# A transformer block on one NeuronCore: 32-row head slots in the Q/K scratch, a DMA model of 16 engines, and an order searched offline

## The chip, the cores and the metric

The kernel runs on one core of a Trainium2 chip. It is written in Bass: the program says itself which instruction each engine runs, in which order, and on which semaphores it waits. The engines are TensorE (PE, matrix products; its weight loads have a row of their own, PEld), VectorE (DVE), ScalarE (ACT), GpSimd (POOL) and SyncE (SP), which here issues every DMA. The metric is the device time of one execution in microseconds (us).

## The reference

One block with sliding-window attention and a gated MLP; the layer norms are modulated by a vector `c`. 2048 rows, width 640, 32 heads of 20, a window of 256 keys, 1536 hidden units.

```python
mod = (silu(c) @ w_mod).reshape(1, 6, 1, 640)        # sa, ca, ga, sb, cb, gb
h = layernorm(x) * (1 + ca) + sa
qkv = h @ wqkv                                       # [2048, 3*640]: q, k, v of 32 heads x 20
scores = q @ k.T * 20 ** -0.5                        # per head
scores = where(0 <= i - j < 256, scores, -1e9)       # causal, sliding window
o = softmax(scores) @ v
x = x + ga * (o @ wo)
h = layernorm(x) * (1 + cb) + sb
x = x + gb * ((sigmoid(h @ w_gate) * (h @ w_up)) @ w_down)
```

## The kernel before

The Python code is a small list scheduler. Every piece of work is an operation `A(engine, function, duration, reads=..., writes=..., prio=..., tag=...)`; buffers are pools of slots that a `Tile` takes when its first operation is placed. `schedule()` simulates the engines with the durations given, takes at each step the operation that can start first (among those that can start within 0.13 of each other on TensorE, the one with the lowest `prio`), and so fixes each engine's order; `emit()` then writes that order with semaphore waits. Nothing is reordered on the chip: each engine runs its list, and waits where an operand is late. For a DMA the model is one shared pipe:

```python
            dur = o.dur[e]
            free[e] = st + dur
            if o.isdma:
                s0 = max(st + dur + 0.3, bw)
                move = o.nbytes / 330e3
                bw = s0 + move
                o.end = s0 + move + o.fix
```

The 2048 rows are 16 blocks of 128. Q, K and V are made in four chunks of four blocks (`cc`); attention, output projection and MLP run over six chunks `a` of 2, 2, 4, 4, 2 and 2 blocks. The buffers that matter here:

```python
    p_stg = sbpool("stg", 3, [128, 512])
    p_QT = sbpool("QT", 3, [128, 4, 512])
    p_KT = sbpool("KT", 4, [128, 4, 512])
    p_V = sbpool("V", 10, [128, H * VW + 10])
    p_E = sbpool("E", 4, [128, 4, 512])
    p_On = sbpool("On", 2, [128, 1024])
    p_oT = sbpool("oT", 1, [128, NDT, 512])
    p_big = sbpool("big", 1, [128, 6400])
# ... PSUM:
    p_S = Pool("S", [nc.alloc_psum_tensor("S0", [128, 4, 512], F32)])
    p_O = Pool("O", [nc.alloc_psum_tensor("O0", [128, 512], F32)])
    p_M = Pool("M", [nc.alloc_psum_tensor(f"M{i}", [128, 512], F32) for i in range(3)])
```

The vector `c` is loaded first, with its 640 values spread over 128 partitions, then x, `w_mod` and the Q/K/V weights:

```python
    dma(lambda: c_col[:], lambda: c.rearrange("o (t p) -> p (o t)", p=128), 1280, writes=[R_ccol], prio=0, nonc=True)
```

hT is the normed and modulated x with the features on the partitions. In chunk 0 TensorE transposes it; in chunks 1 to 3 a DMA transpose does, and VectorE modulates the result in place:

```python
        else:
            for bi in range(4):
                transp(t, src[bi], bi, 4)
            modulate(t, 512, 4, scA, shA, [R_mA], 12)
```

[...] For chunk 0 a *direct* projection makes them so: four heads go to four 32-column parts of the TensorE array, which work side by side (20 matmuls for each group of 4 heads, for each of q and k, for each half `hf` of the chunk):

```python
                    for k0, k1 in ((0, 1), (1, 2), (2, 3), (3, 4), (4, 5)):
                        def fn(e, eng, k0=k0, k1=k1, which=which, ps=ps, g_=g_):
                            for kt in range(k0, k1):
                                for j in range(4):
                                    c0 = kt * D + (4 * g_ + j) * DH
                                    ins = mm(e, ps.ap[32 * j:32 * j + 32, 0:256], wqk_t[which][:, c0:c0 + 32],
                                             hT[0].ap[:, kt, hf * 256:hf * 256 + 256], kt == 0, kt == NDT - 1,
                                             tp=(0, 32 * j))
```

For chunks 1 to 3 plain 128-row projections are used. The result (640 rows) is written to a DRAM scratch from a staging buffer `stg`, and read back with the heads spread out, four reads of 20 partitions each:

```python
    def proj_qk(cc, mts, halves, prio):
        for which, (w, Rw) in enumerate(((wq, R_wq), (wk, R_wk))):
            key = "qk"[which]
            if (cc, which) not in dq:
                dq[(cc, which)] = (dram(f"d{key}{cc}", [D, 512]), [R(f"d{key}{cc}_{m}") for m in range(NDT)])
            dt_, Rd = dq[(cc, which)]
            for mt in mts:
                ps = Tile(p_M, f"{key}{cc}_{mt}")
                pairs = [(lambda kt=kt, mt=mt, w=w, ps=ps: (ps.ap[:], w[:, kt, mt * 128:(mt + 1) * 128],
                                                            hT[cc].ap[:, kt, :])) for kt in range(NDT)]
                s = Tile(p_stg, f"stg{key}{cc}_{mt}")
                pe_chain(ps, 512, pairs, [Rw + [hT[cc].r(kt)] for kt in range(NDT)], prio, f"proj{key}{cc}", hold=[s])
                evac(lambda s=s: s.ap[:], lambda ps=ps: ps.ap[:], 512, [ps.r()], [s.r()], 6, "evqk")
                dma(lambda mt=mt, d=dt_: d[mt * 128:(mt + 1) * 128, :], lambda s=s: s.ap[:], 131072, reads=[s.r()],
                    writes=[Rd[mt]], prio=2, fix=0.9, tag="qkw")
            for hh in halves:
                t = Tile((p_QT, p_KT)[which], f"{key}T{cc}_{hh}")
                (QT, KT)[which][(cc, hh)] = t
                lo, hi = 320 * hh // 128, (320 * hh + 319) // 128
                for j in range(4):
                    dma(lambda j=j, t=t: t.ap[32 * j:32 * j + DH, :, :],
                        lambda j=j, hh=hh, d=dt_: d.rearrange("(g r) c -> r g c", r=4 * DH)[
                            j * DH:(j + 1) * DH, 4 * hh:4 * hh + 4, :], 81920,
                        reads=[Rd[m] for m in range(lo, hi + 1)], writes=[t.r(j)], prio=2, k=10, tag="qkr")
```

Attention goes over the 8 groups of 4 heads. `pieces_of` cuts a group's (key block, query block) pairs into sets of at most four 128-column blocks; one set is one score run on TensorE (into the single score buffer S), one exp on ScalarE, masks of its diagonal and far blocks on GpSimd, and one PV run on TensorE, placed later and in pairs:

```python
    def pieces_of(i0, QB):
        ps = []
        for kb in range(max(0, i0 - 2), i0 + QB):
            q0, q1 = max(kb, i0), min(kb + 2, i0 + QB - 1)
            ps.append((kb, q0, q1 - q0 + 1))
        ps.sort(key=lambda x: (-x[2], x[0]))
        sets = []
        for p in ps:
            for s in sets:
                if sum(y[2] for y in s) + p[2] <= 4:
                    s.append(p)
                    break
            else:
                sets.append([p])
        return sets
        ...
        for g in range(NG):
            hh, gl = g // 4, g % 4
            gpo = 512 // W
            if g % gpo == 0:
                O = Tile(p_O, f"O{a}_{g}")
            first = [True] * 4
            qt = QT[(cc, hh)]
            for si, st in enumerate(sets):
                E = Tile(p_E, f"E{a}_{g}_{si}")
                ...
                    for (kb, q0, n) in st:
                        kt = KT[(kb // 4, hh)]
                        for j in range(4):
                            ins = mm(e, Sp.ap[:, j, off:off + n * 128],
                                     kt.ap[32 * j:32 * j + DH, gl, (kb % 4) * 128:(kb % 4) * 128 + 128],
                                     qt.ap[32 * j:32 * j + DH, gl, (q0 % 4) * 128:(q0 % 4 + n) * 128],
                                     True, True, tp=(32 * j, 0))
```

`norm` transposes the accumulator O with VectorE, divides by the softmax sums and transposes back into On. On then goes to a DRAM scratch `doc` in four stores, one for each head of a group, and comes back as oT in one read:

```python
        out_r = []
        for j in range(4):
            Rj = R(f"doc{a}_{g0}_{j}")
            dma(lambda j=j: doc.rearrange("(g r) c -> r g c", r=4 * DH)[j * DH:(j + 1) * DH, g0:g0 + G, :],
                lambda j=j: On.ap[32 * j:32 * j + DH, :].rearrange("p (g c) -> p g c", g=G), 40960,
                reads=[On.r(0), On.r(1)], writes=[Rj], prio=1, k=10, fix=0.9, tag="n_ow")
            out_r.append(Rj)
        return out_r
# ... and after the last group:
        oT = Tile(p_oT, f"oT{a}")
        dma(lambda: oT.ap[:, :, 0:W], lambda: doc.rearrange("(t p) c -> p t c", p=128), D * W * 2, reads=R_doc,
            writes=[oT.r()], prio=2, tag="oT")
```

The output projection and the MLP follow; `qkv` orders the projections:

```python
    def qkv(cc):
        if cc == 0:
            proj_qk_direct(0, 12)
            proj_v(0, 12.35)
            proj_qk_direct(1, 13.6)
        else:
            proj_qk(cc, (0, 1, 2), (0,), 20 + cc)
            proj_v(cc, 20 + cc)
            proj_qk(cc, (3, 4), (1,), 20 + cc)
# ... the MLP of one chunk, 12 tiles of hidden units, gate and up (W is 256 or 512), then down:
        for ft in range(NFT):
            pg, pu, sg = Tile(p_M, "g"), Tile(p_M, "u"), Tile(p_sig, "sig")
            for ps, w, tg in ((pg, 0, "g"), (pu, 1, "u")):
                pairs = [(lambda kt=kt, ft=ft, ps=ps, w=w: (ps.ap[:, 0:W], wgu[:, w, kt, ft * 128:(ft + 1) * 128],
                                                            h2.ap[:, kt, 0:W])) for kt in range(NDT)]
# ...
                    ps.ap[:, 0:320], hv(ft)[:, bi * 128:(bi + 1) * 128], wd[:, ft, half * 320:half * 320 + 320]))
                    for ft in range(NFT)]
```

The softmax here doesn't subtract the row's maximum and nothing guards it: scores larger than these inputs give would overflow.

## Time and profile before

| | |
|---|---|
| time, median of 3 | 361.11 us (359.8 to 361.29) |
| span of the profiled execution | 358.6 us |
| mean granted TensorE clock | 0.995 |
| exps on ScalarE (128 partitions x 2048, 1536, 1024 elements) | 72, 8 and 24 |
| exp of 128x2048 | 1.876 us |
| direct projection matmuls | 640 |
| DMA packets | 52672, of which 22544 under 512 B |
| moved by DMA | 40.32 MB |

In the profile a line such as `L521` names the line of the kernel; L521 and L522 are the two branches of the matmul helper, without and with a tile position, so that L522 is scores (`S`), PV (`O`) and direct projections. `dq`, `dk` and `doc` are the DRAM scratches, `wgu` and `wd` the MLP weights, `big` the MLP's hidden units (and, early, `w_mod`). A group of instructions shows how many there were, their busy time and the mean time of one, and after a second bar the idle time of the engine just before them, with what ended it. A wait shows total us, how often, and the longest.

The chain that ended last, by share of the span:

```profile
PE 71%; DMA 9%; DVE 7%; SPq 4%; ACT 3%; issue 3%; POOL 1%; DVEq 0%; POOLq 0%
```

The busy time by stage (window, length, then PE, PEld, DVE, ACT and POOL busy with their instructions, clock, DMA share, GB/s):

```profile
0.00:9.00 9.00, 6.40 (x38) 2.83 (x39) 3.61 (x10) 1.49 (x2) 4.30 (x33) 1.00 0.66 204
9.00:54.00 45.00, 41.09 (x988) 27.73 (x986) 35.20 (x80) 32.93 (x44) 24.10 (x35) 1.00 0.81 244
...
280.00:358.60 78.60, 75.60 (x558) 52.95 (x558) 32.87 (x73) 14.95 (x34) 2.17 (x4) 1.00 0.11 28
```

Attention starts at about 15 us and ends shortly after 280; what follows is output projection and MLP of the last chunks.

### The profile page before, as it was taken

The page shows a single profiled execution, that of the slowest core. Times are in us where ns is not written, and L with a number is a line of the kernel's source. Part 1 is how long each engine was busy: PE and PEld are TensorE (multiplying, and loading weights), DVE is VectorE, ACT ScalarE, POOL GpSimd, SP SyncE. Part 2 cuts the span into 40 slices and gives each one's busy share as a digit, 9 for nine tenths or more (in the row PEclk, how much of TensorE's full clock was granted, in tenths as well). Part 3 has the DMA queues.
Part 4 walks back from the last instruction along what each step waited for, and adds up shares of the span by engine and source line. Part 5 has one row for each costly group of instructions (what it writes and reads, how often), then busy time and mean ns, then how long its engine had stood idle before and what let it go on. Part 6 is the DMA issues. An engine that isn't in the chain of part 4 may idle for free.

```text
span 358.6 us, 10125 instructions
## 1 busy us (share of the span) xinstructions
PE 339.7 (95%) x4014; PEld 198.3 (55%) x4038; DVE 233.9 (65%) x504; ACT 223.6 (62%) x231; POOL 182.4 (51%) x304
## 2 busy tenths in 40 slices
PE   7989989989699999999999999999999999999996
PEld 3657556445235564445666534544664454788884
DVE  4569987994678977649787464776677755433342
ACT  1577876768648888887888788678678312022130
POOL 4227855985468975666676565566656201000000
PEclk9999999999989999999999999999999999999999
DMA  6988489696962652431281123003323010310101
GB/s 204 354 295 274 106 185 385 159 194 126 265 208 66 166 80 64 122 118 53 62 140 38 57 74 92 5 20 65 87 89 85 25 42 1 74 38 0 38 1 39
DMA packets 52672, 40.32 MB, mean 112 GB/s; under 512 B 22544, under 2 KB 49424, under 8 KB 52624
## 3 DMA queue, kind: packets, MB, share of 16 engines
q1 hardware_dynamic: 52624, 39.67, 40.7%
q8 instruction: 32, 0.52, 0.6%
q14 instruction: 16, 0.13, 0.1%
HBM read 25.89 MB, written 9.18 MB: 98 GB/s over the span
## 4 chain that ended last, share of the span: by engine, by line
PE 71%; DMA 9%; DVE 7%; SPq 4%; ACT 3%; issue 3%; POOL 1%; DVEq 0%; POOLq 0%
PE M L521 57%; PE S L522 7%; PE O L522 6%; SPq L438 4%; ACT E L802 3%; DMA oT<-doc 2%; DMA dq<-stg 2%; DMA x<-in_A_x_dram 2%; DVE x L602 2%; DMA hT<-x 1%; DMA big<-in_w_mod_dram 1%; PE M L522 1%; PE S L510 1%; DVE T L870 1%; DVE h2T L613 1%
## 5 line engine op out<-in xcount | busy, mean ns | idle before, releaser
L802 ACT ACTIVATE E<-S 128x2048 bf16<-128x2048 f32 (+1 forms) x104 | 171.3, 1647 | 43.2 <-PE S L522 40.4
L818 POOL TENSOR_SCALAR_AFFINE_SELECT E<-E 128x512 bf16<-128x512 bf16 x128 | 82.9, 657 | 84.7 <-ACT E L802 81.5
L521 PE MATMUL M<-h2T,wgu 128*128 128x256 bf16 (+1 forms) x708 | 110.8, 307 | 1.3 <-issue 0.8
L521 PEld LDWEIGHTS M<-h2T,wgu 128*128 128x128 bf16 x720 | 67.1, 98 | 35.5 <-issue 5.7
L820 POOL TENSOR_SCALAR_AFFINE_SELECT E<-E 128x512 bf16<-128x512 bf16 x112 | 73.6, 664 | 0.0
L928 ACT ACTIVATE sig<-M 128x256 f32<-128x256 f32 (+1 forms) x72 | 31.9, 454 | 56.7 <-PE M L521 56.6
L930 DVE SCALAR_TENSOR_TENSOR big<-sig,M 128x256 bf16<-128x256 f32 (+1 forms) x72 | 36.5, 507 | 44.8 <-PE M L521 36.2
L521 PE MATMUL M<-wd,big 128*128 128x320 bf16 x384 | 56.4, 299 | 0.0
L521 PEld LDWEIGHTS M<-wd,big 128*128 128x128 bf16 x384 | 36.5, 98 | 16.5 <-issue 1.9
L522 PE MATMUL S<-QT,KT 20*128 20x256 bf16 (+2 forms) x832 | 38.6, 259 | 3.0 <-ACT E L802 1.9
L522 PE MATMUL O<-E,V 128*32 128x256 bf16 (+2 forms) x832 | 32.4, 263 | 0.7 <-POOL E L818 0.7
L522 PEld LDWEIGHTS S<-QT,KT 20*128 20x128 bf16 x832 | 12.6, 92 | 34.6 <-ACT E L802 20.0
L940 DVE TENSOR_TENSOR x<-M,x 128x320 bf16<-128x320 f32 x32 | 15.6, 488 | 21.4 <-PE M L521 21.2
L870 DVE STREAM_TRANSPOSE T<-O 128x512 f32<-128x512 f32 x32 | 22.7, 711 | 9.6 <-PE O L522 9.0
L591 DVE BATCH_NORM_STATS2 st<-x 128x6 f32<-128x320 bf16 x64 | 27.1, 472 | 1.9 <-DMA x<-in_A_x_dram 1.7
L521 PE MATMUL M<-wo,oT 128*128 128x320 bf16 x160 | 26.1, 300 | 1.2 <-DMA oT<-doc 1.2
L521 PE MATMUL M<-wv,hT 128*128 128x320 bf16 x160 | 25.6, 300 | 1.0 <-DVE hT L651 1.0
L522 PEld LDWEIGHTS O<-E,V 128*32 128x32 bf16 x832 | 15.4, 95 | 15.9 <-issue 7.8
L521 PE MATMUL M<-hT,wk 128*128 128x512 bf16 x70 | 19.2, 398 | 4.1 <-DMA dq<-stg 3.8
L879 DVE STREAM_TRANSPOSE On<-Tn 128x512 bf16<-128x512 bf16 x32 | 22.5, 704 | 0.4
L667 DVE CAST stg<-M 128x512 bf16<-128x512 f32 x19 | 13.1, 690 | 14.3 <-PE M L521 14.2
L602 DVE TENSOR_SCALAR x<-x,st 128x640 bf16<-128x640 bf16 x32 | 19.9, 649 | 2.4 <-POOL st L599 2.3
(59 smaller groups left out, 280.3 us busy)
## 6 DMA issues: line engine op xcount, KB each, us to landing
x<-in_A_x_dram SPq DMA_DIRECT2D x32, 160.0 KB
big<-in_w_mod_dram SPq DMA_DIRECT2D x15, 320.0 KB
doc<-On SPq DMA_DIRECT2D x64, 40.0 KB
out_dram<-x SPq DMA_DIRECT2D x16, 160.0 KB
wgu<-in_B_w_gate_dram SPq DMA_DIRECT2D x5, 384.0 KB
wgu<-in_B_w_up_dram SPq DMA_DIRECT2D x5, 384.0 KB
wd<-in_B_w_down_dram SPq DMA_DIRECT2D x6, 320.0 KB
dq<-stg SPq DMA_DIRECT2D x15, 128.0 KB
```

The lines of the kernel that those rows point to most:

```text
L521: return e.matmul(o, l, r, start=st, stop=sp, skip_group_check=True)
L522: return e.matmul(o, l, r, start=st, stop=sp, tile_position=tp, skip_group_check=True)
L591: ins = e.bn_stats(v(bi * 12 + j * 6, 6), src[bi].ap[:, j * 320:(j + 1) * 320])
L602: A("dve", lambda e, g, bi=bi: e.tensor_scalar(dst[bi].ap[:], src[bi].ap[:], v(48 + 2 * bi, 1), v(60 + bi, 1), op0=ALU.subtract, op1=ALU.m ...
L802: A("act", lambda e, eng, E=E, Sp=Sp, ncol=ncol: e.activation(E.ap[:, :, 0:ncol], Sp.ap[:, :, 0:ncol], ACT.Exp, scale=SM_SCALE), c_act(4 * ...
L818: return e.affine_select(ap, ap, pattern=[[0, 4], [1, 128]], compare_op=ALU.is_ge, fill=0.0, base=0, channel_multiplier=-1)
L820: return e.affine_select(ap, ap, pattern=[[0, 4], [-1, 128]], compare_op=ALU.is_ge, fill=0.0, base=-1, channel_multiplier=1)
L870: A("dve", lambda e, g: e.transpose(T1.ap[:], O.ap[:]), c_dve(512), reads=[O.r()], writes=[T1.r()], prio=4, tag="tr1")
L879: A("dve", lambda e, g: e.transpose(On.ap[:, half * 512:half * 512 + 512], Tn.ap[:]), c_dve(512), reads=[Tn.r()], writes=[On.r(half)], pri ...
L928: A("act", lambda e, g, pg=pg, sg=sg: e.activation(sg.ap[:, 0:W], pg.ap[:, 0:W], ACT.Tanh, scale=0.5), c_act(W), reads=[pg.r()], writes=[s ...
L930: A("dve", lambda e, g, pu=pu, sg=sg, ft=ft: e.scalar_tensor_tensor(out=hv(ft), in0=sg.ap[:, 0:W], scalar=1.0, in1=pu.ap[:, 0:W], op0=ALU. ...
L940: A("dve", lambda e, g, ps=ps, bi=bi, half=half: e.tensor_tensor(x1[bi].ap[:, half * 320:half * 320 + 320], ps.ap[:, 0:320], x1[bi].ap[:, ...
```

## The change

It does several things at once.

- The DRAM scratch of Q and K has 32 rows for each head instead of 20 (the 12 spare rows are filled with zeros once), one scratch for q and one for k for all chunks. Weight columns are taken with a stride of 5, so that a 128-row result holds 4 rows of each head. One read then brings all 128 partitions of four groups. There are six staging buffers instead of three.
- The second half of chunk 0 no longer goes by the direct projection but through the scratch like the other chunks.
- The attention output keeps 32-row slots too: one store of 128 partitions instead of four of 20, and four reads of 32 partitions with long rows. `wo` is loaded with its rows in the matching order.
- hT of chunks 1 and 2 is made by TensorE transposes, with the modulation in the eviction; chunk 3 keeps the DMA transpose.
- In chunks 1, 4 and 5 a set may hold blocks of two head groups.
- `c` is loaded as one row and turned by TensorE.
- The scheduler's DMA model has 16 engines and the time to generate descriptors, durations are set nearer to measured ones, and a table of priority offsets, found by a search offline for an order that bears delays, is added to the priorities. The order on every engine is another one.

The diff, cut:

```diff
+                acc = max(st + 0.1, dge)
+                free[e] = max(st + dur, acc + 0.3)
+                dge = acc + 0.0018 * o.nd
+                last_ = 0.0
+                for i in range(o.k):
+                    eng16[i] = max(acc + 1.15, eng16[i]) + o.nd / o.k / 1e3 * (9 + o.nbytes / o.nd / 27.2)
+                    last_ = max(last_, eng16[i])
+                bw = max(bw, last_)
...
+PRIO = {
+    "dma": 42, "wm0": 48, "wqk": 114.5, "x2": 103, "wv": 66.75, "pad": -36.5, "stats@l0": 9.75, "aggr@l0": 9.5,
+    "ptr@l0": -92.25, "hT0@l0": 5, "projd@q0": 0.25, "projv0@q0": 0.75, "evv@q0": 5.25, "projq0@q0": -67.5,
+    ...  (63 more offsets)
...
-    p_stg = sbpool("stg", 3, [128, 512])
+    p_stg = sbpool("stg", 6, [128, 512])
-    dma(lambda: c_col[:], lambda: c.rearrange("o (t p) -> p (o t)", p=128), 1280, writes=[R_ccol], prio=0, nonc=True)
+    A("pool", lambda e, g: e.memset(one[:], 1.0), 0.1, writes=[R_one], prio=0)
+    c_row = p_On.aps[0][0:1, 0:D]
+    dma(lambda: c_row, lambda: c, 1280, writes=[R_crow], prio=0, nd=1, k=1)
...
+    def fc(e, g):
+        for t in range(NDT):
+            ins = mm(e, ps_c.ap[:, t:t + 1], c_row[:, t * 128:t * 128 + 128], one[:], t == 0, True)
+        return ins
...
+        elif cc in PET:
+            for dt in range(NDT):
+                ps = Tile(p_M, "tr")
+
+                def fn(e, g, dt=dt, ps=ps):
+                    for bi in range(4):
+                        ins = mm(e, ps.ap[:, bi * 128:(bi + 1) * 128], src[bi].ap[:, dt * 128:(dt + 1) * 128], ident[:],
+                                 bi == 0, True)
+                ...
+                A(("act", "dve"), ev, {"act": 0.75, "dve": 0.72}, reads=[ps.r(), R_mA], writes=[t.r(dt)], prio=5, tag="hTe")
...
+        d_ = dram(f"d{k}", [32 * H, 512])
+        Rp = R(f"pad{k}")
+        dma(lambda d=d_: d.rearrange("(h r) c -> h r c", r=32)[:, DH:32, :],
+            lambda: zr[0:H, 0:1, :].to_broadcast([H, 12, 512]), 12288 * H, writes=[Rp], extra=[o_z],
+            prio=13, tmin=10.0, tag="pad", bg=True, nd=384, wr=True)
...
+                    ps.ap[:, 0:cw], w[:, kt, mt:D:NDT], hT[cc].ap[:, kt, c0:c0 + cw]))
+                    for kt in range(NDT)]
+                ...
+                dma(lambda mt=mt, d=d_: bass.AP(d.tensor, d.offset + mt * 512, [[32 * 512, H], [NDT * 512, 4], [1, cw]]),
+                    lambda s=s: s.ap[:, 0:cw], 256 * cw, reads=[s.r()],
+                    writes=[Rd[mt]], prio=2, wr=True, dur=0.6, tag="qkw")
+            ...
+                if cw == 512:
+                    dma(lambda t=t: t.ap[:], lambda hh=hh, d=d_: d.rearrange("(g p) c -> p g c", p=128)[
+                        :, 4 * hh:4 * hh + 4, :], 524288, reads=Rd + [Rp], writes=[t.r("r")], prio=2, tag="qkr", nd=512)
...
+    def pieces_of(i0, QB, gs):
         ps = []
         for kb in range(max(0, i0 - 2), i0 + QB):
             q0, q1 = max(kb, i0), min(kb + 2, i0 + QB - 1)
-            ps.append((kb, q0, q1 - q0 + 1))
-        ps.sort(key=lambda x: (-x[2], x[0]))
+            for g in gs:
+                ps.append((g, kb, q0, q1 - q0 + 1))
+        ps.sort(key=lambda x: (-x[3], x[0], x[1]))
         sets = []
 ...
+            if a == 0:
+                sets = [x for g in gs for x in pieces_of(i0, QB, [g])]
+            else:
+                sets = pieces_of(i0, QB, gs)
...
+        for q in range(4):
+            dma(lambda q=q: oT.ap[32 * q:32 * q + 32, 0:NDT * W].rearrange("p (t c) -> p t c", t=NDT),
+                lambda q=q: doc.rearrange("(h r) c -> h r c", r=32)[:, 5 * q:5 * q + 5, :], 320 * W, reads=R_doc,
+                writes=[oT.r(q)], prio=2, tag="oT", nd=32)
...
-        out_r = []
-        for j in range(4):
-            Rj = R(f"doc{a}_{g0}_{j}")
-            dma(lambda j=j: doc.rearrange("(g r) c -> r g c", r=4 * DH)[j * DH:(j + 1) * DH, g0:g0 + G, :],
-                lambda j=j: On.ap[32 * j:32 * j + DH, :].rearrange("p (g c) -> p g c", g=G), 40960,
-                reads=[On.r(0), On.r(1)], writes=[Rj], prio=1, k=10, fix=0.9, tag="n_ow")
-            out_r.append(Rj)
-        return out_r
+        Rj = R(f"doc{a}_{g0}")
+        dma(lambda: doc.rearrange("(g p) c -> p g c", p=128)[:, g0:g0 + G, :],
+            lambda: On.ap[:].rearrange("p (g c) -> p g c", g=G), 262144, reads=[On.r(0), On.r(1)], writes=[Rj], prio=1,
+            nd=128 * G, wr=True, tag="n_ow")
+        return [Rj]
...
-            proj_qk_direct(1, 13.6)
+            proj_qk(0, 12.7, 256, 256)
         else:
-            proj_qk(cc, (0, 1, 2), (0,), 20 + cc)
-            proj_v(cc, 20 + cc)
-            proj_qk(cc, (3, 4), (1,), 20 + cc)
-
...
+    wo_src = A_wo.rearrange("(h q t) f -> q h t f", h=H, t=NDT)
+    R_wol = [R(f"wol{q}") for q in range(4)]
+    for q in range(4):
+        dma(lambda q=q: wo[32 * q:32 * q + 32, :, :], lambda q=q: wo_src[q], 204800, writes=[R_wol[q]], prio=30,
+            tmin=12.0, tag="wo", bg=True, nd=32)
```

The kernel before, as the reader of the diff sees it, and the one after do the same arithmetic on the same inputs, apart from the order of sums in the output projection.

## The prediction

> **What bounds the kernel now.** First the page's busy shares, then the span in 40 slices.

> ```profile
> span 358.6 us, 10125 instructions
> PE 339.7 (95%) x4014; PEld 198.3 (55%) x4038; DVE 233.9 (65%) x504; ACT 223.6 (62%) x231; POOL 182.4 (51%) x304
> ...
> PE   7989989989699999999999999999999999999996
> ...
> DMA  6988489696962652431281123003323010310101
> ```

> TensorE looks full, but its ends are modelled, so I ask what matmuls cost where nothing disturbs them. Near the end of the timeline (start, length, engine, instruction, count):

> ```profile
> 335.97 13.26 PE L521 MATMUL M<-h2T,wgu 128*128 128x256 bf16 x120
> ...
> 349.07 6.68 PE L521 MATMUL M<-wd,big 128*128 128x320 bf16 x48
> ```

> In the groups a 256-column matmul is 0.273 us long, though the next starts much sooner; a run so ends about 0.17 us late, and a 256-column matmul costs (13.26-0.17)/120 = 0.109 us and a 320-column one 0.136. Ten 512-column ones took 2.33 us, 0.216 each. The packed ones by their start-to-start times: a run of 20 direct projections 0.55; a full score run (4 blocks) 0.33, a half one 0.22; a full PV run 0.28, a half one 0.16.

> With the instruction counts: gate and up 480 x 0.109 + 240 x 0.216 = 104.2; down 384 x 0.136 = 52.2; output projection and V 320 x 0.136 = 43.5; Q/K 150 x 0.216 = 32.4; direct 32 x 0.55 = 17.6; scores 72 full, 24 half, 8 of three blocks (0.28) = 31.3; PV likewise 25.6; modulation and transposes 10. Sum 317. The first useful matmul starts at 6.15 us and the last ends 2.8 us before the span does: 326. So about 32 us of 358.6 are waits and restarts, and nearly all lie before 280: the chain of work ends in one unbroken TensorE piece (start, length).

> ```profile
> 300.29 55.48 PE M L521 x446
> ```

> **Whatever time TensorE gets back earlier therefore comes off the end.**

> Where the waits are: the view of waits for PE, and the largest in the timeline.

> ```profile
> PE M L521 <- DMA dq<-stg: 3.8, 2, 3.2
> ...
> PE M L521 <- DMA oT<-doc: 1.2, 2, 0.8
> PE M L521 <- DVE hT L651: 1.0, 1, 1.0
> PE S L522 <- DMA KT<-dk: 0.9, 1, 0.9
> ...
> PE M L522 <- DVE QT L667: 0.6, 1, 0.6
> ```

> ```profile
> 98.80 2.19 PE L521 MATMUL M<-hT,wk 128*128 128x512 bf16 x6 [3.24 <-DMA dq<-stg]
> ```

> That matmul waits for a staging buffer: the write that empties it took 5.23 us in the chain (93.43 to 98.66). And the pause costs twice; windows (length, PE busy, clock, DMA share, GB/s):

> ```profile
> 95.50:98.80 3.30, 0.06 (x5) 1.00 1.09 308
> 99.80:103.20 3.40, 3.40 (x23) 0.50 0.47 148
> ```

> TensorE runs at half clock for 3.4 us, another 1.7 us. The rest is mode changes, which show as waits of the weight loads on "issue" and on the exp:

> ```profile
> PEld M L521 <- issue: 20.2, 80, 3.5
> PEld S L522 <- ACT E L802: 20.0, 56, 0.7
> ```

> [...] a score run among wide matmuls has weight-load idle of 0.2 to 0.4 us beside it. [...] here the first 0.9 us of traffic (1.9 to 2.8) is 359 packets under 512 B that move 0.00 MB.

> **The change, part by part.**
> 1. *Staging 3 to 6 buffers, one issue per Q/K read, one per attention store.* A staged tile costs TensorE 5 x 0.216 = 1.1 us, and attention work lies between tiles, so three more tiles outlast the 5.23 us landing. Gone: 3.8 + 1.7 = **5.5 us**.
> 2. *Blocks of two head groups share a score buffer* (chunks 1, 4 and 5, of 2 blocks). Each pair of groups had 2 full and 2 half sets and now has 3 full. So 24 + 24 sets become 36: 104 runs fall to 92, scores to 84 x 0.33 + 8 x 0.28 = 30.0 (-1.3), PV to 25.1 (-0.5). PV runs go in pairs, so 12 score runs and 6 PV pairs stop breaking wide work; at an estimated 0.15 us for restarting (of the 0.2 to 0.4 of idle above), 2.7. Together **4.5 us**. On ScalarE, two half exps become one full one twelve times, 12 x (2 x 1.023 - 1.876) = 2.0 us less, beside TensorE:

> ```profile
> L802 ACT ACTIVATE E<-S 128x2048 bf16<-128x2048 f32 x72 | 135.1, 1876 | 32.4 <-PE S L522 30.6 <-POOL E L818 1.5
> ...
> L802 ACT ACTIVATE E<-S 128x1024 bf16<-128x1024 f32 x24 | 24.6, 1023 | 9.5 <-PE S L522 8.6
> ```

> 3. *The second half of chunk 0's Q/K no longer direct.* 16 runs x 0.55 = 8.8 go, 50 x 0.109 = 5.5 come: -3.3, and some mode changes, **-4**. The new trip through DRAM is read only by chunk 1, over 20 us later.
> 4. *hT of chunks 1 and 2 by TensorE.* 40 transposes of 128 columns, some 0.06 us each, **+2.4**, and 10 evictions of 0.6 to 0.7 us on ScalarE or VectorE for 10 modulations of 0.51 on VectorE. Eight DMA transposes go.
> 5. *Output of attention.* Four stores of one output tile held SyncE 1.3 to 2.9 us; one store should hold it about 0.4. The oT read of 640 rows becomes four of 32 longer rows. Of the oT, KT, QT and hT waits (1.2 + 0.9 + 0.6 + 1.0 = 3.7) I take **2.5** off.
> 6. *c as one row*: the 0.9 us of tiny packets stand ahead of the x and modulation loads, which then move without a break; **0.8**.
> 7. *The searched order.* Windows again:

> ```profile
> 54.00:126.00 72.00, 65.78 (x704) 0.98 0.72 195
> 126.00:280.00 154.00, 150.80 (x1742) 1.00 0.30 73
> ```

> 6.2 us of TensorE idle in the first, of which part 1 has 3.8, against 3.2 us in the second, twice as long. I give the search **2** more, and take **2** back for what it may misjudge.

> Sum: 5.5 + 4.5 + 4 - 2.4 + 2.5 + 0.8 + 2 - 2 = 14.9 us; 361.1 - 14.9 = **346 us**.

> **Rivals.** (a) *A new wait takes the place of the old.* Q and K now have one scratch for all chunks, so a chunk's writes wait until the last chunk's reads are done, and these wait for K buffers. Rows grow from 20 to 32: 12 reads of 512 KB for 48 of 80 KB, 16 stores of 256 for 64 of 40, and 0.8 MB of padding; with chunk 0's second half about 6 MB on 40 MB. For: the DMA share is 0.81 in 9 to 54 and 0.72 in 54 to 126. Against: it is 0.30 after 126. If the staging stall moves instead of going: 353. (b) *ScalarE and the single score buffer set the pace.* A full set is an exp of 1.876 plus scores and signals, some 2.4 us; 72 such, 24 of 1.55 and 8 of 2.0 make 226 us of the 265 during which scores run. It is close to a bound, and TensorE fills the holes; with 84 and 8 it is 218, so it eases. If the searched order starves it, attention ends later and the dense tail shrinks without gain: 351. (c) *The search finds most of the 32 us.* Head and tail excepted, half of it could go beyond my sum: 338. (d) *The offline order fits its model, not the chip*: every engine runs a fixed order, so a late load (the Q/K weights are put last in the first group) stops all behind it; 360 or more.

> **Range and chances.** Parts 1, 2 and 3 rest on counts and an observed stall, 14 us before the transposes; if half of the rest fails I am at 350, and (a) and (b) lie at 351 to 353. Range 337 to 356. Faster by over 2% means under 353.9: 0.83. Within 2%: 0.13. Slower: 0.04.

> **What would show it.** Right: no wait of wk or wq matmuls on dq<-stg or dk<-stg and no window at half clock after 10 us; 92 exps, 84 of 128x2048; 320 direct matmuls; 60 transposes on ident; no packets ahead of x; attention's end at about 265 to 270 with the dense tail unbroken after it. PE busy near 330. Wrong: a new PE wait over 2 us on KT<-dk, QT<-dq or weights; DMA share about 1 between 9 and 54 with TensorE idle; exps ending after 280.

## The result and the profile after

The kernel after takes **346.8 us** (median; 346.5 to 347.3), 0.960 of the time before [0.955, 0.965]. The profiled execution spans 344.8 us where before it spanned 358.6. The page of the kernel after, its busy times and its DMA packets:

```profile
span 344.8 us, 9578 instructions
PE 334.3 (97%) x3787; PEld 200.5 (58%) x3813; DVE 230.2 (67%) x498; ACT 225.4 (65%) x225; POOL 176.8 (51%) x300
...
DMA packets 50989, 44.98 MB, mean 130 GB/s; under 512 B 16513, under 2 KB 46850, under 8 KB 50946
```

Span less TensorE's busy time is its idle time: 18.9 us before, 10.5 after. So of the 13.8 us between the two profiles 8.4 are waits that are gone, and 5.4 are busy time, of which 1.7 is the stretch that ran at half clock before. (Both traces lack some matmul records, 24 before and 26 after, counted against the weight loads. Records of 512 columns are 0.380 us long on average and start 0.216 apart where nothing disturbs them, so a missing one leaves a gap of some 0.05 us, and by this estimate up to about 1 us of either idle time is not real.) Where the idle time went is read from the same stages as before (window, length, PE busy with its matmuls, clock, DMA share, GB/s):

```profile
9.00:54.00 45.00, 42.60 (x723) 1.00 0.71 212
54.00:126.00 72.00, 70.77 (x836) 1.00 0.83 238
126.00:280.00 154.00, 152.53 (x1713) 1.00 0.36 94
```

TensorE's idle time falls from 3.9 to 2.4 us in the first stage, from 6.2 to 1.2 in the second, from 3.2 to 1.5 in the third. The DMA engines are busier than before from 54 us on (0.83 for 0.72, then 0.36 for 0.30) and move 4.7 MB more, and yet TensorE waits less. What is left of the waits for PE, and of the weight loads':

```profile
PE M L545 <- DMA dq<-stg: 0.6, 1, 0.6
PE S L546 <- ACT E L887: 0.4, 2, 0.2
```

```profile
PEld S L546 <- ACT E L887: 17.2, 49, 0.6
PEld M L545 <- issue: 15.6, 72, 0.8
```

The staging wait is 0.6 us for 3.8. The two weight-load waits beside mode changes (from plain to packed matmuls or back) were 20.0 and 20.2; 53 of the 56 on the exp and 73 of the 80 on issue stood at such a change before. They shrink with the number of score runs. The exps now (group: busy, mean ns, idle before):

```profile
L887 ACT ACTIVATE E<-S 128x2048 bf16<-128x2048 f32 x84 | 157.6, 1877 | 30.6 <-PE S L546 25.3 <-POOL E L900 3.3 <-POOL E L898 1.6
```

84 full ones, and 8 of 128x1536, as counted. The chain still ends in one unbroken piece of TensorE work, which starts earlier:

```profile
284.65 57.20 PE M L545 x454
```

It began at 300.29 before. The last score matmul is at 263.5 us, and no stretch between 7 us and the last microseconds is at half clock.

At the full clock, where matmuls of one kind follow each other, 128-column ones start 0.056 us apart (the transposes on ident in the kernel after) and 512-column ones 0.216: 384 columns more in 0.160 us, or 2.4 columns per ns. From one four of packed direct matmuls (256 columns each) to the next it is 0.109 us, the same as from one plain 256-column matmul to the next. Summing columns over all matmuls at that rate, four packed ones counted as one, gives by this estimate 295.9 us of TensorE work before and 294.8 after (taken from two runs below that do the same work and whose traces lack no record: the kernel before with six staging buffers, and the kernel after in plain order). **The arithmetic hardly shrank.** What differs is how it is joined together: in order of their starts the matmuls change 266 times between scores, PV, direct and wide ones where they changed 297 times, and there are fewer waits. From 126 to 268 us the first start after a change between plain and packed comes, by the medians of both traces, 0.09 to 0.10 us later than the columns ahead of it take; between plain ones in one chain 0.00.

### The profile page after: what moved, and what is told of

Same layout as the page of the kernel before. It is cut to its first block, busy times and chain, and to the rows that moved or that the text cites. A ratio compares the mean times of both kernels' runs of the same rounds, so it can differ in the third digit from the quotient of the medians.

```text
span 344.8 us, 9578 instructions
## 1 busy us (share of the span) xinstructions
PE 334.3 (97%) x3787; PEld 200.5 (58%) x3813; DVE 230.2 (67%) x498; ACT 225.4 (65%) x225; POOL 176.8 (51%) x300
## 4 chain that ended last, share of the span: by engine, by line
PE 83%; DMA 5%; DVE 3%; ACT 2%; issue 2%; POOL 2%; SPq 2%; DVEq 0%
PE M L545 66%; PE S L546 8%; PE O L546 7%; DMA wk<-in_A_wqkv_dram 3%; ACT E L887 2%; SPq L467 2%; PE M L546 2%; DMA x<-in_A_x_dram 1%; DMA dq<-stg 1%; POOL E L900 1%; DVE x L640 1%; POOL E L898 1%; DVE hT L708 0%; DVE T L948 0%; DVE st L629 0%
## 5 line engine op out<-in xcount | busy, mean ns | idle before, releaser
L887 ACT ACTIVATE E<-S 128x2048 bf16<-128x2048 f32 (+1 forms) x92 | 169.2, 1840 | 31.6 <-PE S L546 26.2
L898 POOL TENSOR_SCALAR_AFFINE_SELECT E<-E 128x512 bf16<-128x512 bf16 x128 | 86.7, 681 | 35.9 <-ACT E L887 34.6
L900 POOL TENSOR_SCALAR_AFFINE_SELECT E<-E 128x512 bf16<-128x512 bf16 x112 | 73.5, 663 | 41.4 <-ACT E L887 41.2
L1003 ACT ACTIVATE sig<-M 128x256 f32<-128x256 f32 (+1 forms) x72 | 32.4, 454 | 56.4 <-PE M L545 55.7
L546 PE MATMUL S<-QT,KT 20*128 20x256 bf16 (+2 forms) x832 | 36.2, 258 | 0.8 <-ACT E L887 0.4
L1015 DVE TENSOR_TENSOR x<-M,x 128x320 bf16<-128x320 f32 x32 | 15.6, 488 | 23.4 <-PE M L545 23.4
L546 PE MATMUL O<-E,V 128*32 128x256 bf16 (+2 forms) x832 | 31.0, 261 | 0.3 <-DVE T L948 0.3
L545 PE MATMUL M<-wv,hT 128*128 128x320 bf16 x160 | 24.8, 300 | 0.3 <-ACT hT L706 0.2
L546 PEld LDWEIGHTS O<-E,V 128*32 128x32 bf16 x832 | 14.5, 95 | 15.6 <-issue 9.9
L545 PE MATMUL M<-hT,wk 128*128 128x512 bf16 (+1 forms) x94 | 20.2, 353 | 1.2 <-DMA dq<-stg 0.6
L545 PE MATMUL M<-hT,wq 128*128 128x512 bf16 (+1 forms) x94 | 20.8, 354 | 0.5 <-issue 0.2
L640 DVE TENSOR_SCALAR x<-x,st 128x640 bf16<-128x640 bf16 x32 | 17.7, 588 | 4.2 <-POOL st L637 4.2
```

Of the source, the lines that this page charges most:

```text
L545: return e.matmul(o, l, r, start=st, stop=sp, skip_group_check=True)
L546: return e.matmul(o, l, r, start=st, stop=sp, tile_position=tp, skip_group_check=True)
L640: A("dve", lambda e, g, bi=bi: e.tensor_scalar(dst[bi].ap[:], src[bi].ap[:], v(48 + 2 * bi, 1), v(60 + bi, 1), op0=ALU.subtract, op1=ALU.m ...
L887: A("act", lambda e, eng, E=E, Sp=Sp, ncol=ncol: e.activation(E.ap[:, :, 0:ncol], Sp.ap[:, :, 0:ncol], ACT.Exp, scale=SM_SCALE), c_act(4 * ...
L898: return e.affine_select(ap, ap, pattern=[[0, 4], [1, 128]], compare_op=ALU.is_ge, fill=0.0, base=0, channel_multiplier=-1)
L900: return e.affine_select(ap, ap, pattern=[[0, 4], [-1, 128]], compare_op=ALU.is_ge, fill=0.0, base=-1, channel_multiplier=1)
```

## The experiments

The prediction's sum was close, so the question is whether its terms were. *Theory*: the gain is the sum of the parts, as priced. *Rivals*: the searched order brings most of it; or the staging stall alone explains the kernel before.

A schedule is made offline, so every edit also moves the order of everything after it. The offsets of the searched order were found for one kernel. Most edits are therefore made to the kernel after **without the offsets** ("plain order"). Ratios are to the kernel before, timed beside each, with a 95% interval; a difference of two ratios times 361 us gives the us quoted between kernels. No edit leaves work of the block out. Where the time at half clock is given for several executions, it is an estimate, from the 0.50 that the clock reads in such a stretch: twice the share of the clock that was not granted, times the span.

### The kernel before, with six staging buffers

```
-    p_stg = sbpool("stg", 3, [128, 512])
+    p_stg = sbpool("stg", 6, [128, 512])
```

> The kernel before with six staging buffers instead of three, nothing else (the order is scheduled anew). Theory A, the sum of the prediction: the stall on dq<-stg (3.24 us, and 0.5 us more elsewhere) and the 1.7 us lost to the half clock go, nothing takes their place: 361.2 - 5.5 = about 355.7 us, no window at half clock. Rival B, the order decides: the loads and transposes still collide between 90 and 100 us, another wait of 2 us or more stands there: 359 to 362 us.

Measured: 366.0 us, 1.0105 [1.0075, 1.0135] of before: slower. No matmul waits for a staging buffer any more, and TensorE stops at the same place for another reason. The chain of waits from 91.7 us (start, length):

```profile
91.74 4.81 DMA x<-in_A_x_dram
...
96.98 0.47 DVE st L591
97.46 0.63 DVE T L870
...
98.22 0.40 PE O L522 x8
```

A load of x lands after 4.81 us. VectorE takes its instructions in a fixed order, and a layer-norm statistic of that x stands ahead of the transpose `T` that frees the single PV accumulator, so PV matmuls wait 3.0 us, and a half-clock stretch of 3.41 us follows (98.97 to 102.38) in place of the one at 99.81. Another of 6.8 us comes later. It is outside both ranges that were expected, but the wait of Rival B is there. What follows: more buffers alone, with the order made anew, move the stall and do not remove it. In that stage loads and writes land late (this x after 4.81 us, the write of the kernel before after 5.23; 0.72 of the DMA engines' time is taken there before), and here it is VectorE's list, with a late landing in front of the transpose, that stops TensorE. My rival (a) happens, but to this half-change, not to the whole.

### The same, scheduled with the 16-engine model

The edit is the one above plus the DMA model of the change in `schedule()`, with the engines and descriptors of the old transfers (for instance `k=10, nd=80` for a 20-row read); no work is altered.

> The kernel before with six staging buffers and the scheduler's new DMA model (16 engines, descriptor time[...]), every transfer shaped as before; no offsets. Six buffers alone measured 366.0 us, a stall of 3.0 us at 95 us moved on to a load of x that landed 4.8 us late. Theory C: that stall comes from an order made with a wrong idea of when loads land; with the new model the loads are placed where they land in time: 355 to 359 us, no half clock. Rival B: the model alone does not change it, the congestion comes from the transfers' shapes: 362 us or more, with a wait of 2 us or more between 85 and 105 us.

Measured: 360.3 us, 0.9951 [0.9915, 0.9988]. The better model alone takes about 5.6 us off the kernel with six buffers (1.0105 to 0.9951), and brings it slightly under the kernel before. That is between the two ranges expected, and half clock remains (3.6 to 7.2 us in every execution): an order made with the better model is better, but not free of stalls; scores wait 5.4 us in all on exps.

### The kernel after in plain order

```
-        o.prio = prio + PRIO.get(o.grp, 0.0)
+        o.prio = prio
```

> The changed kernel without the table of offsets that the search found (every priority as written, the DMA model kept). Theory A: the parts carry the gain and the search was worth about 2 us: 348 to 350 us. Rival B: the search carries most of it, the parts alone little: 354 us or more, with new TensorE waits of several us.

Measured: 353.3 us, 0.9745 [0.967, 0.9819]. So the offsets are worth 0.9745 - 0.9598 = 0.0147, 5.3 us (6.6 by the medians), and everything else 9.2 us; by the intervals each is good to some 3 us. No stretch at half clock. The same stage as above:

```profile
54.00:126.00 72.00, 68.41 (x788) 1.00 0.80 245
```

3.6 us of idle where the searched order has 1.2; scores wait 3.6 us in all on the exp, 0.4 with the offsets:

```profile
PE S L546 <- ACT E L887: 3.6, 8, 1.3
```

Rival (d), an order that fits the model and not the chip, is refuted: on the chip too the searched order is better than the plain one.

### How far is any order from another: shifted priorities

```
+        o.prio = prio + (0.0 if eng == "sp" else random.Random(f"{o.grp}/4").uniform(-0.3, 0.3))
```

> The same work as the kernel without the offsets (353.3): the priorities of groups of compute operations are shifted by random amounts up to 0.3, so that the order is another one and nothing else. Theory D (an untuned order is worth several us either way): 350 to 360 us, other waits and perhaps a window at half clock. Theory A (the order matters little as long as the work is the same): 352 to 355 us.

Measured: 354.9 us, 0.9805 [0.9755, 0.9855]: 2.2 us over plain order, which the intervals do not tell from nothing, although only 36% of the places in TensorE's list hold the same kind of instruction as there. This is a single draw and no bound on what order can do: the offsets alone moved the kernel by 5.3 us, the model alone the kernel before by 5.6, and the model row of the table below, where no work differs either, by 8.3. A single term below that size is not told from a change of order.

### Taking one part away from the plain order

Three staging buffers (`p_stg` 6 to 3):

> The changed kernel without the offsets and with three staging buffers again. Against the one without the offsets, Theory A: the stall comes back, about 5 us slower, wk or wq matmuls waiting on dq<-stg or dk<-stg. Rival B: other waits set that stage, within 1.5 us of the one without the offsets.

Sets of one head group again:

```
-            if a == 0:
+            if True:
                 sets = [x for g in gs for x in pieces_of(i0, QB, [g])]
```

> The changed kernel without the offsets, and sets that hold blocks of one head group alone, as before (104 score runs and exps instead of 92). Against the one without the offsets, Theory A: 4.5 us slower (1.8 of packed matmul time, 2.7 of restarts). Rival B: TensorE waits elsewhere meanwhile, under 2 us slower.

The second half of chunk 0 direct again:

```
-            proj_qk(0, 12.7, 256, 256)
+            proj_qk_direct(1, 13.6)
```

> The changed kernel without the offsets, chunk 0's second half by the direct projection again (640 direct matmuls, no trip through DRAM for chunk 0). Against the one without the offsets (353.3), theory A (part 3 of the prediction): 4 us slower, of which 3.3 us are matmul time. Rival: the early stage waits for loads anyway, under 1.5 us slower.

Every Q/K read and attention store as four transfers of 20 rows (20 of the 32 rows of a slot, the slots kept):

```
-                if cw == 512:
+                if False:
...
+        for j in range(4):
+            dma(lambda j=j: doc.rearrange("(g p) c -> p g c", p=128)[32 * j:32 * j + DH, g0:g0 + G, :], ...
```

> The changed kernel without the offsets, with the slots kept, but every Q/K read and every store of the attention output again as four transfers of 20 rows (84 issues more; the spare rows are not moved). Against the one without the offsets (353.3), theory A (part 5 and the title's claim): the fewer, wider transfers matter, 2 to 4 us slower. Rival: with attention work of other groups in between the landing is hidden, within 1 us.

The shared-pipe DMA model instead of the 16 engines:

> The changed kernel's work and transfers, scheduled with the old model of one shared pipe for DMA and without the offsets (the durations of compute operations stay the new ones). Theory A: the new shapes carry the gain, the model little: within 2 us of the kernel without offsets (353.3). Theory C: the order suffers from the wrong landing times: 356 to 362 us, with waits on loads or on operations behind a load.

hT of chunks 1 and 2 by DMA transpose and VectorE:

```
-PET = (1, 2)
+PET = ()
```

> The changed kernel without the offsets, hT of chunks 1 and 2 by DMA transposes and VectorE again. Against the one without the offsets (353.3): theory A (part 4 of the prediction, only TensorE work counts): 2.4 us faster, about 351. Rival: eight DMA transposes of 160 KB and the in-order engines behind them cost more than the matmul time they save: 355 us or more, hT<-x among the waits.

Measured:

| taken away | us | ratio to before | over plain order, us | at half clock, us (median; range) |
|---|---|---|---|---|
| nothing (plain order) | 353.3 | 0.9745 [0.967, 0.9819] | | 0 (0 to 0.7) |
| three of six staging buffers | 358.8 | 0.9899 [0.9827, 0.9972] | 5.6 | 10 (10 to 14) |
| shared sets | 359.3 | 0.9930 [0.9902, 0.9959] | 6.7 | 3.6 (0 to 7.1) |
| wide transfers | 360.7 | 0.9973 [0.9945, 1.0000] | 8.2 | 10.7 (3.6 to 18) |
| 16-engine model | 361.8 | 0.9976 [0.9942, 1.0010] | 8.3 | 6.5 (0 to 10.9) |
| scratch for chunk 0's second half | 362.4 | 1.0032 [1.0006, 1.0058] | 10.4 | 3.6 (0 to 10.2) |
| transposes by TensorE | 369.1 | 1.0180 [1.0131, 1.0228] | 15.7 | 23.9 (21 to 25) |

Executions over 1.5% above the fastest of their kernel are left out, which bears mainly on the row of the 16-engine model: ten of its twenty are such, and with them its median is 364.1.

Each part costs more to lose than I had priced it, by the middle of its interval; but they sum to 55 us where the whole of them brings 9. They are not terms of a sum. Since each row is also another order, and the model row shows 8.3 us with no work altered, no row shows what its own part is worth; only the last is larger than every change that order alone made to plain order. (The model row lies in Theory C's range, the last in its rival's; no time lies within a rival's "under 1.5" or "within 1 us".) Part of each loss is half clock. At half clock up to half of the time is lost (in the kernel before, 512-column matmuls start 0.43 us apart there and 0.216 elsewhere), so by this estimate up to 12 of the 15.7 us in the last row, 5 of the 5.6 in the first, but only 1.8 of 6.7 and of 10.4. Without shared sets eight of twenty executions had the full clock throughout, and they took 357.0 to 359.6 us, still some 5 us over plain order.

With three staging buffers nothing waits for a staging buffer, though the prediction's reason was that wait. In its order scores wait on exps instead (6.3 us in all against 3.6; timeline, in brackets the idle time ahead and its releaser). After the first of these two pauses the clock falls, and the second comes at half clock:

```profile
107.32 0.40 PE L546 MATMUL S<-QT,KT 20*128 20x384 bf16 x8 [1.55 <-ACT E L887]
...
112.30 0.61 PE L546 MATMUL S<-QT,KT 20*128 20x256 bf16 x8 [1.99 <-ACT E L887]
```

```profile
104.90:108.30 3.40, 1.81 (x36) 0.99 0.32 120
108.30:118.50 10.20, 6.39 (x64) 0.50 0.78 252
```

With the DMA transposes the chain of waits shows a new cost, in SyncE's own row (`SPq`), before the landing:

```profile
63.56 1.27 SPq L646
...
64.88 1.27 SPq L646
...
66.19 2.65 DMA hT<-x
```

A DMA transpose holds SyncE's queue 1.27 us against 0.50 for a plain load of x (four in 1.99 us at 69.24 in the same row), and this kernel has twelve of them for hT where plain order has four. The hT they make is late (one matmul waits 2.9 us for its modulation):

```profile
64.70:68.10 3.40, 1.17 (x36) 0.99 0.80 176
68.10:74.80 6.70, 4.72 (x40) 0.50 0.95 298
```

### Narrow transfers with the order held fixed

The edit that removes the objection of the moved order: the searched order of the kernel after is kept instruction for instruction, and only the 12 Q/K reads and 16 attention stores are each written as four transfers of 20 rows on the same semaphore (84 more DMA instructions).

```
-                    dma(lambda t=t: t.ap[:], ...
+                    dma(lambda j, t=t: t.ap[32 * j:32 * j + DH, :, :], ..., parts=4)
```

> The changed kernel with its order kept exactly on every engine; only the 12 Q/K reads of 512 KB and the 16 stores of 256 KB go out as four transfers of 20 rows each, one behind the other, in the same place of SyncE's list (84 issues more; the spare rows are not moved). Without a tuned order the same edit cost 7 us, but there the order changed too. Theory A (the wide transfers matter by themselves): 2 to 4 us slower than the changed kernel (346.8), SyncE issuing later and matmuls or scores waiting on KT<-dk, QT<-dq or doc. Theory D (the order made the 7 us, the landings are hidden): within 1 us of 346.8.

Measured: 352.3 us, 0.9737 [0.9691, 0.9782]: 5.0 us over the kernel after (5.5 by the medians; good to some 2.4). The profiled execution, the fastest of four (351.5), has no half clock; the other three had 3.5 to 7 us of it. SyncE's row of this kernel, and then of the kernel after, at the same reads (start, length, engine, what, count):

```profile
63.82 3.60 SPq L467 DMA_DIRECT2D QT<-dq  x8
...
68.55 2.74 SPq L471 DMA_DIRECT2D x<-in_A_x_dram  x3
```

```profile
61.43 1.08 SPq L467 DMA_DIRECT2D QT<-dq  x2
...
64.81 1.63 SPq L467 DMA_DIRECT2D x<-in_A_x_dram  x3
```

Eight issues hold SyncE 3.60 us, two 1.08. It also came to these reads 2.4 us late already, and a store behind them took 1.1 us less; the x loads go out 3.7 us later. The load itself is no slower, 3.85 us to its landing here and 4.75 there. From there the way is that of the first experiment: VectorE has the statistics of that x in front of an eviction of V, stands 4.13 us instead of 1.45 (the second line is of the kernel after), and TensorE waits behind it.

```profile
72.42 1.68 DVE L633 BATCH_NORM_STATS2 st<-x 128x6 f32<-128x320 bf16 x4 [4.13 <-DMA x<-in_A_x_dram]
...
69.58 1.68 DVE L629 BATCH_NORM_STATS2 st<-x 128x6 f32<-128x320 bf16 x4 [1.45 <-DMA x<-in_A_x_dram]
```

```profile
PE M L549 <- DVE V L727: 2.6, 1, 2.6
```

In 70 to 75 us TensorE is busy 2.4 us here and 4.8 in the kernel after: that is half of the 4.9 us between the two spans; the other half is not traced to single issues. No wait of a matmul for K, Q or oT shows with the narrow transfers either. All DMA issues together hold SyncE 156 us here and 131 in the kernel after. What follows: as far as it is traced, the wide transfers pay by the instructions that SyncE no longer has to issue. (Over the whole change SyncE gains little, 136 us of issues before for 131: the new scratch adds others.) How many of the 16 DMA engines a transfer used no view shows, and these runs don't separate it: the narrow reads also move fewer bytes.

### Searching on

The experiments say that order, not work, is where time still lies. The same search, carried on for an hour from the table of the change, with nothing else edited:

```
-PRIO = { ... }   (77 offsets)
+PRIO = { ... }   (236 offsets)
```

> The kernel after with another table of offsets: the same random search was carried on for an hour from the table of the change, with the scheduler of the change and a replay in which every transfer lands late by a random amount (0.6 us on average). Nothing of the work is altered. Theory that the order matters through waits and half clock, and that these are nearly used up (10.5 us of TensorE idle left, over half of it at the head and the tail): the new order bears delays slightly better, so 345.5, between 344 and 348. Rival, that the search is far from done and its model true to the chip: 342 or less. Rival, that what is left between orders is fit to the model and not to the chip: 348 to 353, with waits of 1 to 2 us that the table of the change doesn't have, perhaps a half-clock stretch.

Measured: 347.1 us (346.1 to 347.8), 0.9578 [0.9535, 0.9621]: the same as the kernel after. TensorE's idle time reads 9.1 us (span 345.9, busy 336.8) for 10.5, but this trace lacks no matmul record and the other lacks 26, which is most of that difference. TensorE's list parts from that of the kernel after at its 202nd instruction and holds another kind of matmul in 15% of its places; the two orders end within their scatter. None of the versions that ran beats the kernel after.

## Why the prediction was right, by its steps

**The total, the range and what was to be seen held.** 346 was said, 346.8 came. No stretch at half clock; 92 exps, 84 of them full; 320 direct matmuls; 60 transposes on ident; the last exp's end at 265.6 (265 to 270 said); the dense tail unbroken; no packets ahead of x; PE busy 334.3 (near 330 said); waits on dq<-stg once, 0.6 us, instead of never. The reading that carried it is the first: some 32 us of waits and restarts ahead of a dense tail, so that anything recovered comes off the end.

**The terms were much less right than their sum.**

1. *Staging, 5.5*: taking three buffers away costs 5.6, which is the size but not the mechanism: no matmul waits for a buffer there either. Adding them alone made the kernel slower by 3.8 us. I took the wait that the profile names for the resource that is short; it was the place where late DMA landings met TensorE in that order. The step that failed is "three more tiles outlast the 5.23 us landing. Gone": the wait went, and another came. The 1.7 us for half clock is about right as a size: seven executions of the kernel before, of all that were timed beside these runs, that had the full clock throughout took 360.3 us on average, 53 with 0.995 of it 361.5.
2. *Shared sets, 4.5*: 6.7 to undo, some 5 in the executions without half clock. The counts (104 runs to 92) are exact, and the weight-load waits fell by 2.8 and 4.6 us between the kernels before and after. That fits the 4.5, but the undone kernel is another order too, and a change of order is as large.
3. *Chunk 0's second half, 4*: 10.4 to undo, and two executions without half clock still took 360.1 and 361.2 us, 7 to 8 over plain order. At least one gap of 3.3 us, inside a score run, has no cause in the records. Its size stays open.
4. *TensorE transposes, +2.4*: **the sign was wrong, as far as the runs show.** The 40 added transposes cost TensorE about what I said (128 columns, 0.056 us from start to start, 2.2 in all), but without them the plain order loses 15.7 us, nearly twice the most that order alone changed from there (8.3). I priced the TensorE time added and gave no worth to the eight DMA transposes removed, each 1.27 us of SyncE and a late hT. How much of the 15.7 is the order, no run tells.
5. *Wide transfers, 2.5*: 5.0 with the order fixed. Right mechanism (issue time of SyncE), wrong place: I counted the waits for Q, K, oT and hT themselves. These are nearly gone after (0.4 of 3.7 us, all of it hT), but those for Q, K and oT do not come back with narrow transfers; the cost falls on what stands behind in SyncE's queue, here x.
6. *c as one row, 0.8*: nothing that the trace shows (no run takes it alone). Of 441 packets under 512 B in the first 2.9 us 20 are left and data moves from 1.9 us on, but three x loads and the row of c now stand ahead of `w_mod`, whose first issue moved from 2.33 to 2.56 us, and the last of the first modulation's matmuls start at 10.55 us, 10.61 before. A cheaper item at the head of a queue helped only the next items, not the one that is waited for.
7. *The order, 2 for the search and -2 for misjudging*: 5.3 for the offsets, and the DMA model 5.6 to 8.3 beside them. These are changes of order with the work as it was, so this term was mis-sized; its idle time is in the windows (54 to 126: 6.2 before, 3.6 plain, 1.2 searched).

So the order and, as it seems, the transposes brought more than I gave them, and the staging buffers as such and the row of c brought less. That these errors cancel in the sum is luck: what the runs support is the budget of idle time, not my division of it.

**The rivals.** (a), a wait that takes the stall's place, is what the staging buffers alone do, and what the whole doesn't: with 4.7 MB more traffic TensorE waits less than before. (b) ScalarE did ease: scores' weight loads wait less on exps, and attention ends earlier. (c) was nearer for the search than I gave it, but the waits at the front and in mode changes stayed (15.6 us of weight loads on issue). (d) is refuted by the plain order, which is slower. That searching on gave nothing more also speaks against (c)'s 338.

## What to carry to other kernels

With every engine's order fixed, the wait that a profile names is where late work met the engine, not what made it late: ask what else stands in the same queues and would be next, and expect a single buffer or queue fix to move the stall. Count DMA instructions as time on the engine that issues them (0.45 us each for the narrow reads here), and look at what stands behind them. Where an edit also remakes the order, leave-one-out costs are not terms of a sum, and one that is no larger than a change of order alone says nothing of its part: hold the order fixed where the edit allows it. The idle time by stage tells how much there is to win.

## What the runs showed of the hardware

```profile
72.90:76.30 3.40, 1.76 (x37) 1.00 0.70 219
```

What separates the two in these traces is the matmul work, counted as above, in columns at 2.4 per ns with four packed matmuls as one: 0.36 of the window in the first, 0.43 in the second. Over the traces of this study but one (the shared-pipe model's), 15 windows at full clock that were followed by half clock held 0.01 to 0.38 by this count; of over 1200 others, leaving out each run's last microseconds, the lowest held 0.39. The edge is no finer than the count, which has to split matmuls between windows. So the window ahead need not be idle; what the hardware counts is not shown.

**A weight load with a stride** of 5 elements takes 119 ns in the kernel after against 98 ns for a dense one; it lay beside matmuls and cost nothing that shows (256-column matmuls start 109 ns apart with either).
